# Merged DMAs, earlier query copies and another queue order in an attention and feed-forward kernel

## The chip, the cores and the metric

The kernel runs on one core of one Trainium2 chip. The metric is the device time of one execution in microseconds (us). A core has TensorE (matmuls; PE in the profile, PEld its weight loads), VectorE (DVE), ScalarE (ACT), GpSimd (POOL) and SyncE, whose queue (SP) issues the DMAs of this kernel.

## The reference

```python
def _attn_ref(q, k, v):              # q, k, v: 8 x 8 x 1152 x 64
    B, H, S, D = q.shape
    q_pool = q.reshape(B, H, S // 2, 2, D).mean(axis=3)
    scores = 1.0 / np.sqrt(D) * np.matmul(q_pool, k.transpose(0, 1, 3, 2))
    scores = scores - np.max(scores, axis=-1, keepdims=True)
    attn = np.exp(scores)
    attn = attn / (np.sum(attn, axis=-1, keepdims=True) + 1e-09)
    return np.matmul(attn, v)

def _moe_ref(x, w_in, w_out):        # x: 4608 x 512, w_in: 512 x 2048
    h = x @ w_in
    g = h - np.tanh(h)
    return g @ w_out
```

The attention's output, its heads side by side, is the x of the feed-forward part. Neighbouring queries are averaged in twos, so a head has 576 queries and 1152 keys. The maximum that is subtracted is the true one of each row.

## The kernel before

The attention stage comes first and the feed-forward stage after it. The attention works on 32 pairs of heads (8 batches, 4 pairs each). A pair is 36 units: for two halves of 288 queries, three groups of three key blocks of 128, and two heads, one unit multiplies a key block with 288 queries (two matmuls into one PSUM tile `ps_s`, of which there are three) and takes the exponential into `p_f`. The scores come out transposed, keys on partitions, so the row maximum must be known before: it is carried by two more rows (64 and 65) of the second operand `t2`.

These maxima are found ahead, by matmuls of their own. `query_sums` adds the two queries, `hi_part` (ScalarE) and `lo_part` (VectorE) split queries and keys into a high and a low part. `max_queries` copies the high queries by DMA into `bd`, a block-diagonal operand of 9 tiles of 128 columns, one buffer for even and one for odd pairs. `max_part` multiplies tiles of it with a third of the keys into `ps_m` (two buffers), and VectorE reduces that to `mx`; a pair has 14 such parts. `max_rows` reduces `mx` to the row maxima (`nm`), splits them (`m2`), has TensorE transpose them, ScalarE copy them (`mt`), one DMA write them to `m_dram` and others bring them back into `t2`. `operands` copies the high and low parts into the score operands `t1` and `t2` with ten DMAs, 2.6 MB a pair in all.

Behind the scores, GpSimd adds three of a group's `p_f` tiles (`z_part`), TensorE multiplies `p_f` with v (`pv`), and `z_sums` multiplies the sums with ones, 32 columns wide, to give the softmax's denominators. At the end of a batch these go through `z_dram`, `reciprocals` (VectorE) and `spread` to `r_dram`; the second stage multiplies x by them. Beside this `w_block` splits the weights into high and low parts, a block every 34 units, in steps on ScalarE, VectorE and GpSimd, and stores them in `wi_dram` and `wo_dram`.

All of this is ordered by hand. `add(u, f)` puts a step on the list of unit u; `run(u, first)` runs the list `first` ahead of the unit's score, `run(u)` the list `at` behind it, and `pv` follows. The units of each step are given relative to the first unit of its pair, so -35 is 35 units before the pair begins. Engines keep this order: an instruction that waits holds up all behind it on its engine, and SyncE's queue holds all DMAs of the stage. The dictionary `units`, with the lists `parts` and `rows`, holds the places; pairs 0, 1 and 2 have places of their own. In the steady part of the stage the places of one pair in terms of the pair that is computed are: load at 16 and query sums at 33 (three pairs ahead), high parts at 35, 1 and 3, bd copies at 4, low parts at 8, 10 and 12, maxima from 15 on, over 31 units; and for the next pair operands at 1, v at 6, row maxima at 15, their store at 21 and return at 26.

The feed-forward stage takes ten chunks (eight of 512 tokens, two of 256) through 16 blocks of the hidden dimension; its loops are not part of the change.

Of the kernel before, what the change touches and what calls it, by code (L numbers as in the profile page):

```python
# [8 lines left out]
F32 = mybir.dt.float32  # L9
# [34 lines left out]
def kernel(  # L44
# [18 lines left out]
    P = 128  # L63
# [73 lines left out]
    with ExitStack() as actx:  # L137
# [45 lines left out]
        def load(pi):  # L183
            w = pairs[pi] = Pair()
            w.b, w.hp = divmod(pi, NP)
            w.i = pi % 2
            w.q_n = ld.tile([P, 2, SQ], F32, name="q_n")
# [45 lines left out]

        spots = [((j, j + 4), (c,)) for c in range(3) for j in range(4)] + [((8,), (0, 1)), ((8,), (2,))]

        def max_part(u, pi, ts, cs):

            w = pairs[pi]
            ps = ps_m.tile([P, 2, 512], F32, name="ps_m")
            both = [(t, c) for t in ts for c in cs]  # L240
            for i, (t, c) in enumerate(both):
                pe.matmul(ps[:, i, 0:CH], bd[w.i][:, t * P:(t + 1) * P], w.hi[:, SQ + c * CH:SQ + (c + 1) * CH], start=True, stop=True)
            mx = w.mx[:, ts[0]:ts[-1] + 1:4, cs[0]] if len(ts) == 2 else w.mx[:, 8, cs[0]:cs[-1] + 1]
            add(u + 1, lambda: dve.tensor_reduce(mx, ps[:, 0:len(both), 0:CH], axis=AX.X, op=ALU.max))

        def max_rows(u, pi, ta, tb):

            w = pairs[pi]
            n = tb - ta
            c0, c1 = ta * P, min(tb, 4) * P  # L250
            nm = sm.tile([P, 2, 5], F32, name="nm")[:, :, 0:n]
            dve.tensor_reduce(nm[:, :, 0:min(tb, 4) - ta], w.mx[:, 0:8].rearrange("p (h t) c -> p h t c", h=2)[:, :, ta:min(tb, 4)],
                              axis=AX.X, op=ALU.max, negate=True)
            if tb == 5:
                dve.tensor_reduce(nm[:, :, n - 1], w.mx[:, 8:9].broadcast_to([P, 2, 3]), axis=AX.X, op=ALU.max, negate=True)
            m2 = sm.tile([P, 20], F32R, name="m2")[:, 0:4 * n].rearrange("p (s h t) -> p s h t", s=2, h=2)
            dve.tensor_copy(m2[:, 0], nm)
            dve.tensor_tensor(m2[:, 1], nm, m2[:, 0].bitcast(F32), op=ALU.subtract)
            ps = ps_m.tile([P, 2, 512], F32R, name="ps_m")[0:4 * n, 0, 0:P]
            mt = sm.tile([20, P], F32R, name="mt")[0:4 * n]  # L260
            md = m_dram[w.i][:, :, ta:tb]

            def turn():
                pe.transpose(ps, m2.rearrange("p s h t -> p (s h t)"), ident_r)

            def out():
                act.activation(mt, ps, AF.Copy)
                add(u + (6 if pi > 1 else 3), lambda: sp.dma_start(md.rearrange("s h t n -> (s h) t n"), mt.bitcast(F32)))

            def back():  # L270
                x2 = t2[w.i].bitcast(F32)
                sp.dma_start(x2[64:66, :, c0:c1], m_dram[w.i][:, :, ta:min(tb, 4)].rearrange("s h t n -> s h (t n)"))
                if tb == 5:
                    for h in range(2):
                        sp.dma_start(x2[64:66, h, 512:SQ], m_dram[w.i][:, h, 4, h * 64:h * 64 + 64])
            add(u + 2, turn)
            add(u + 3, out, at=first)
            add(u + (11 if pi > 1 else 5), back)

# [10 lines left out]
        class Group:  # L290
            pass

        def z_part(grp):
# [5 lines left out]
        def pv(u, grp):  # L299
# [65 lines left out]
        def w_block(u, kind, r, c):  # L365
# [25 lines left out]
            for i, op in ((12, begin),  # L391
                          (14, lambda: ts(whole(t[0]), whole(t[0]), -top, top, op0=ALU.max, op1=ALU.min)),
                          (17, lambda: ts(t[1], t[0], -0x80000000, None, op0=ALU.bitwise_and)),
                          (19, lambda: stt(t[1], t[0], 3, t[1], op0=ALU.logical_shift_left, op1=ALU.bitwise_or)),
                          (22, lambda: ts(t[2], t[1], -0x800000, None, op0=ALU.bitwise_and)),
                          (24, lambda: stt(whole(t[2]), lo, 2.0 ** -36, whole(t[2]), op0=ALU.mult, op1=ALU.mult)),
                          (26, lambda: pool.tensor_tensor(whole(t[1]), whole(t[1]), whole(t[2]), op=ALU.add)),
                          (31, lambda: act.activation(t[3][:, 0], whole(t[1]), AF.Copy)),
                          (33, lambda: pool.tensor_tensor(t[3][:, 1], whole(t[1]), whole(t[3][:, 0]), op=ALU.subtract)),
                          (37, store)):  # L400
                add(u + i, op)
# [28 lines left out]
        for pi in range(n_pair):  # L430
            u = pi * U
            units = dict(load=-92, query_sums=-75, hi_q=-73, hi_k=-71, max_queries=-68, lo_q=-64, lo_k=-62, operands=-35, load_v=-30)
            rows = [(-21, 0, 5)]
            parts = [-57 + i * 34 // 14 for i in range(14)]
            order, step = spots, 2
            if pi == 2:
                units.update(query_sums=-62, hi_q=-60, hi_k=-59, max_queries=-57, lo_q=-54, lo_k=-52)
                parts = [-50 + i * 27 // 14 for i in range(14)]
            if pi < 2:
                order, step = sorted(spots, key=lambda x: x[0][0] in (3, 8)), 0  # L440
            if pi == 0:
                units.update(load=-60, query_sums=-50, hi_q=-49, hi_k=-48, max_queries=-47, lo_q=-46, lo_k=-45, operands=-44,
                             load_v=-43)
                rows = [(-20, 0, 3), (10, 3, 5)]
                parts = [-40 + 2 * i for i in range(9)] + [2 * i for i in range(5)]
            if pi == 1:
                v0 = -U
                units.update(load=v0 - 10, query_sums=v0 - 2, hi_q=v0 - 1, hi_k=v0, max_queries=v0 + 1, lo_q=v0 + 2, lo_k=v0 + 3)
                parts = [v0 + 10 + i * 18 // 14 for i in range(14)]
                units.update(operands=-30)  # L450
                rows = [(-8, 0, 3), (-7, 3, 5)]
            add(u + units["load"], load, pi)
# [5 lines left out]
            add(u + units["max_queries"], max_queries, pi)  # L458
            for x, part in zip(parts, order):
# [3 lines left out]
            for x, ta, tb in rows:  # L463
                add(u + x, max_rows, u + x, pi, ta, tb)

# [157 lines left out]
```

## Time and profile before

| | |
|---|---|
| median of 3 runs | 1932.51 us (1932.48 to 1935.91) |
| profiled execution | 1932.55 us |
| its span, first to last instruction | 1930.8 us |
| mean granted TensorE clock | 0.972 |
| PE busy | 1787.9 us (93%) |
| DVE busy | 1418.0 us (73%) |
| ACT busy | 1094.7 us (57%) |
| POOL busy | 1067.6 us (55%) |
| exponentials, ACT | 1152 of 411 ns |
| maxima, DVE, two tiles | 416 of 955 ns |

Busy time of PE is modelled, since matmuls overlap. Line L37 is a helper through which every instruction of the attention stage passes, so this stage is read by the names of the tiles: `ps_s<-t` is a score, `ps_m<-x,bd` a maximum's matmul, `ps_o<-p_f,v` the product with v, `ps_s<-z,ones` the sums of p, `bd<-x` the copy of the queries, `t<-x` and `t<-kq_l` the operand copies, `t<-m_dram` the return of the row maxima. "SPq" is the DMA-issuing queue: its rows show the time from the first issue to the end of the last. In a timeline the bracket behind a row is the idle time of that engine before it and what ended it. A window's row gives, for each engine, busy time and count, then the granted clock (1.00 is full), the DMA engines' share and GB/s.

### The profile page before, as it was taken

How to read it: one execution, taken by the hardware profiler on the slowest of the kernel's cores; microseconds unless marked ns; L12 is line 12 of the kernel's file. 1: busy time of each engine (PE TensorE's matmuls, PEld its weight loads, DVE VectorE, ACT ScalarE, POOL GpSimd, SP SyncE). 2: the span in 40 equal slices, each digit the busy share in tenths (PEclk: the TensorE clock that was granted, in tenths of full speed). 3: DMA queues.
4: the chain of work that ended last, by engine and by line, in shares of the span. 5: the costliest groups of instructions: out<-in, count | busy, mean ns of one | idle time of the engine just before them, and what ended most of it. 6: DMA issues, size and time to landing. Idle time of an engine off the chain costs nothing.

```text
span 1930.8 us, 28611 instructions
## 1 busy us (share of the span) xinstructions
PE 1787.9 (93%) x9922; PEld 1319.7 (68%) x9922; DVE 1418.0 (73%) x1821; ACT 1094.7 (57%) x2471; POOL 1067.6 (55%) x768
## 2 busy tenths in 40 slices
PE   5799898989899999999899799999999999999998
PEld 3466565656566666666566476787878778788887
DVE  5667665565757676766665089999899889888887
ACT  2355454545545555555455365666666666666676
POOL 2467675757656776766577627443535252524332
PEclk9999999999999999999999899999999999999999
DMA  7567676676757776768675372101101020101000
GB/s 196 130 195 196 181 190 192 175 192 175 211 159 182 200 197 186 195 186 198 184 187 149 133 285 62 54 21 46 40 27 61 6 66 1 58 1 44 9 29 23
DMA packets 110553, 242.33 MB, mean 126 GB/s; under 512 B 24512, under 2 KB 49744, under 8 KB 110408
## 3 DMA queue, kind: packets, MB, share of 16 engines
q1 hardware_dynamic: 110408, 240.50, 45.4%
q8 instruction: 79, 1.29, 0.3%
q14 instruction: 66, 0.54, 0.1%
HBM read 109.64 MB, written 36.42 MB: 76 GB/s over the span
## 4 chain that ended last, share of the span: by engine, by line
PE 60%; DVE 12%; DMA 12%; ACT 5%; POOL 5%; SPq 3%; issue 2%; DVEq 0%; POOLq 0%; ACTq 0%
PE ps_s L37 16%; PE ps_o L37 14%; PE ps_h L521 12%; PE ps_o L546 11%; PE ps_m L37 7%; DMA bd<-x 4%; SPq L37 3%; DMA x_f<-x_dram 2%; DVE g_s L536 2%; DVE g_w L535 2%; DVE g_s L537 2%; ACT p_f L37 2%; DMA x_r<-r_dram 2%; POOL x L120 2%; DVE mx L37 1%
## 5 line engine op out<-in xcount | busy, mean ns | idle before, releaser
L37 ACT ACTIVATE p_f<-ps_s 128x288 f32<-128x288 f32 x1152 | 419.3, 411 | 363.6 <-PE ps_s L37 329.0
L37 DVE TENSOR_REDUCE mx<-ps_m 128x2 f32<-128x768 f32 x448 | 410.4, 926 | 287.5 <-PE ps_m L37 286.4
L37 PE MATMUL ps_s<-t 128*128 128x288 f32 (+1 forms) x2304 | 457.5, 316 | 28.4 <-DMA t<-m_dram 16.1
L37 PEld LDWEIGHTS ps_s<-t 128*128 128x128 f32 (+1 forms) x2304 | 356.9, 193 | 165.9 <-issue 115.3
L37 POOL TENSOR_TENSOR z<-p_f 128x576 f32<-128x576 f32 x192 | 284.2, 1480 | 303.4 <-ACT p_f L37 250.7
L539 POOL TENSOR_TENSOR g_lo<-g_s,g_hi 128x512 fp32r<-128x512 f32 (+1 forms) x160 | 210.6, 1316 | 403.9 <-ACT g_hi L538 344.7
L37 PE MATMUL ps_o<-p_f,v 128*64 128x288 f32 x2304 | 343.7, 437 | 0.0
L521 PE MATMUL ps_h<-x,wi 128*128 128x512 f32 (+1 forms) x1440 | 325.1, 370 | 0.0
L37 PE MATMUL ps_m<-x,bd 128*128 128x384 f32 x864 | 247.9, 363 | 70.3 <-DMA bd<-x 57.5
L37 POOL TENSOR_TENSOR z<-z,p_f 128x576 f32<-128x576 f32 x192 | 297.0, 1547 | 17.7 <-ACT p_f L37 2.9
L521 PEld LDWEIGHTS ps_h<-x,wi 128*128 128x128 f32 x1440 | 254.8, 188 | 51.8
L546 PE MATMUL ps_o<-wo,g_hi 128*128 128x512 f32 x1008 | 275.5, 392 | 4.6 <-ACT g_hi L538 4.2
L37 PEld LDWEIGHTS ps_o<-p_f,v 128*64 128x64 f32 x2304 | 156.2, 144 | 123.2 <-issue 52.0
L546 PEld LDWEIGHTS ps_o<-wo,g_hi 128*128 128x128 f32 x1008 | 186.7, 188 | 46.8 <-ACT g_hi L538 7.9
L37 PEld LDWEIGHTS ps_m<-x,bd 128*128 128x128 f32 x864 | 149.5, 200 | 89.7 <-issue 45.5
L538 ACT ACTIVATE g_hi<-g_s 128x512 fp32r<-128x512 f32 (+1 forms) x160 | 94.3, 589 | 163.6 <-DVE g_s L537 161.2
L532 DVE SCALAR_TENSOR_TENSOR g_w<-g_u,ps_h 128x512 f32<-128x512 f32 (+1 forms) x160 | 100.1, 626 | 99.1 <-PE ps_h L521 67.4
L534 DVE SCALAR_TENSOR_TENSOR g_w<-g_w,g_u 128x512 f32<-128x512 f32 (+1 forms) x160 | 172.8, 1080 | 0.0
L546 PE MATMUL ps_o<-wo,g_lo 128*128 128x512 f32 x504 | 160.1, 393 | 6.6 <-POOL g_lo L539 6.4
L527 ACT ACTIVATE g_u<-ps_h 128x512 f32<-128x512 f32 (+1 forms) x160 | 87.6, 548 | 119.1 <-PE ps_h L521 118.9
L537 DVE COPY_PREDICATED g_s<-g_m,g_t 128x512 f32<-128x512 int32 (+1 forms) x160 | 135.2, 845 | 14.7 <-DVE g_s L536 0.5
L536 DVE SCALAR_TENSOR_TENSOR g_s<-g_s,g_w 128x512 f32<-128x512 f32 (+1 forms) x160 | 131.6, 823 | 17.0 <-ACT g_t L528 0.5
(60 smaller groups left out, 1933.8 us busy)
## 6 DMA issues: line engine op xcount, KB each, us to landing
t<-x SPq DMA_DIRECT2D x64, 432.0 KB
q_n<-in_q_dram SPq DMA_DIRECT2D x32, 576.0 KB
kq<-in_k_dram SPq DMA_DIRECT2D x32, 576.0 KB
t<-kq_l SPq DMA_DIRECT2D x64, 288.0 KB
t<-x SPq DMA_DIRECT2D x64, 288.0 KB
v<-in_v_dram SPq DMA_DIRECT2D x32, 576.0 KB
t<-kq_l SPq DMA_DIRECT2D x64, 144.0 KB
t<-x SPq DMA_DIRECT2D x64, 144.0 KB
```

The lines of the kernel that those rows point to most:

```text
L37: ins = self.tc.keep_in_program_order(f(*args, **kwargs))
L120: pool.tensor_tensor(x_l[:, hp, 0:n], x[:, 0:n], x_h[:, hp, 0:n].bitcast(F32), op=ALU.subtract)
L521: nc.tensor.matmul(h, wi[fc][:, w, c], x[:, c, 0:n], start=(j == 0), stop=(j == len(mm) - 1))
L527: nc.scalar.activation(u, h, AF.Square)
L532: nc.vector.scalar_tensor_tensor(w, u, -P0, h, op0=ALU.add, op1=ALU.mult)
L534: nc.vector.scalar_tensor_tensor(w, w, PL, u, op0=ALU.mult, op1=ALU.mult)
L535: nc.vector.scalar_tensor_tensor(w, s2, P2, w, op0=ALU.add, op1=ALU.mult)
L536: nc.vector.scalar_tensor_tensor(s1, s1, P1, w, op0=ALU.add, op1=ALU.mult)
L537: last = nc.vector.copy_predicated(s1, m.bitcast(I32), th).ins
L538: nc.scalar.activation(g_h, s1, AF.Copy)
L539: nc.gpsimd.tensor_tensor(g_l, s1, g_h.bitcast(F32), op=ALU.subtract)
L546: nc.tensor.matmul(po[j], g[:, ts], wo[fc][:, w], start=(fc == 0 and i == 0), stop=(fc == NF - 1 and i == 2))
```

## The change

The parts, in words:

- `bd` is laid out as two stretches of 576 columns, so that a head's queries are copied by one DMA instead of two; tile 4 holds the last 64 queries of one head and the first 64 of the other.
- `m_dram` has a row of twice 704 numbers, so that one DMA brings the maxima back instead of three. `z_dram` is written by one DMA instead of four, a block of `wi_dram` by one instead of four.
- The places move: for the pair three ahead load at 10, query sums at 22, high parts at 26, 28 and 30, bd copies at 32, low parts at 34 and then 0 and 2 of the following pair, maxima from 12 on over 30 units; operands stay at 1, v at 6; row maxima at 10, transposed at 15, stored at 18, returned at 24.
- A maximum's reduction goes on the list `first` of the unit behind its matmuls.
- `z_sums` is called right behind the next `pv` instead of one unit earlier.
- The reciprocals of a batch come 10 units later, the steps of a weight block 3 units later behind the first.
- Pair 0 finds all maxima before its first unit, and pair 1 is loaded right behind pair 0; both have their bd and operand copies before unit 0 and their row maxima in one go.

```diff
-    m_dram = dram.tile([2, 2, 2, 5, P], F32, name="m_dram")
+    m_dram = dram.tile([2, 2, 2 * (5 * P + 64)], F32, name="m_dram")
...
-                raw_copy(bd[w.i][r, h * 512:(h + 1) * 512], w.hi[r, 0:512])
-                raw_copy(bd[w.i][r, 8 * P + h * 64:8 * P + (h + 1) * 64], w.hi[r, 512:SQ])
+                raw_copy(bd[w.i][r, h * SQ:(h + 1) * SQ], w.hi[r, 0:SQ])
...
-        spots = [((j, j + 4), (c,)) for c in range(3) for j in range(4)] + [((8,), (0, 1)), ((8,), (2,))]
+        spots = [((j, j + 5), (c,)) for c in range(3) for j in range(4)] + [((4,), (0, 1)), ((4,), (2,))]
...
-            add(u + 1, lambda: dve.tensor_reduce(mx, ps[:, 0:len(both), 0:CH], axis=AX.X, op=ALU.max))
+            add(u + 1, lambda: dve.tensor_reduce(mx, ps[:, 0:len(both), 0:CH], axis=AX.X, op=ALU.max), at=first)
...
+        def max_rows(u, pi, steps):
+            w = pairs[pi]
+            nm = sm.tile([P, 2, 5], F32, name="nm")
+            for h in range(2):
+                dve.tensor_reduce(nm[:, h], w.mx[:, 4 * h:4 * h + 5], axis=AX.X, op=ALU.max, negate=True)
...
+            def there():
+                sp.dma_start(md[:, 0:10 * P].rearrange("s (r n) -> s r n", n=P), mt.bitcast(F32))
             def back():
+                sp.dma_start(w.t2[64:66, :, 0:SQ].bitcast(F32), md.rearrange("s (h n) -> s h n", h=2)[:, :, 0:SQ])
+            add(u + steps[0], turn)
+            add(u + steps[0] + 1, out, at=first)
+            add(u + steps[1], there)
+            add(u + steps[2], back)
...
             if grp.g == 2:
                 add(u + 1, o_out, w, hf, at=first)
-                add(u + G - 1, z_sums, u + G - 1, w, hf)
+                late.append((w, hf))
+                if w is pairs.get(n_pair - 1) and hf.n == 1:
+                    add(u + G, lambda: z_sums(u + G, *late.pop()))
+            elif late:
+                z_sums(u, *late.pop())
...
-                    for r in range(4):
-                        sp.dma_start(z_dram[w.b, r // 2, r % 2, w.hp:w.hp + 1], w.z_s[32 * r:32 * r + 1])
+                    sp.dma_start(z_dram[w.b].rearrange("r h a s -> (r h) a s")[:, w.hp], w.z_s[0:P:32])
...
-                        add(u + 12, lambda: reciprocals(dve, *tot[0]))
-                        add(u + 15, lambda: spread(sp, *tot.pop(0)))
+                        add(u + 22, lambda: reciprocals(dve, *tot[0]))
+                        add(u + 25, lambda: spread(sp, *tot.pop(0)))
...
-                    for j in range(0, WB, P):
-                        sp.dma_start(wi_dram[(c + j) // P, :, :, r], src[:, :, j:j + P])
+                    f = c // P
+                    sp.dma_start(wi_dram[f:f + WB // P, :, :, r].rearrange("f p s m -> p s f m"),
+                                 src.rearrange("p s (f m) -> p s f m", m=P))
...
-            units = dict(load=-92, query_sums=-75, hi_q=-73, hi_k=-71, max_queries=-68, lo_q=-64, lo_k=-62, operands=-35, load_v=-30)
-            rows = [(-21, 0, 5)]
-            parts = [-57 + i * 34 // 14 for i in range(14)]
...
+            units = dict(load=-98, query_sums=-86, hi_q=-82, hi_k=-80, max_queries=-76, lo_q=-74, lo_k=-72, operands=-35, load_v=-30)
+            row, steps = -26, (5, 8, 14)
+            parts = [-60 + i * 33 // 14 for i in range(14)]
+            step = 2
             if pi == 0:
...
+                units.update(load=-70, query_sums=-60, hi_q=-59, hi_k=-58, max_queries=-57, lo_q=-56, lo_k=-55, operands=-54,
+                             load_v=-50)
+                row, steps, step = -32, (2, 4, 5), 0
+                parts = [-46 + i for i in range(14)]
             if pi == 1:
                 v0 = -U
...
+                units.update(load=v0 - 69, query_sums=v0 - 31, hi_q=v0 - 30, hi_k=v0 - 29, max_queries=v0 - 28, lo_q=v0 - 27,
+                             lo_k=v0 - 26, operands=v0 - 25)
+                parts = [v0 + 2 + i * 20 // 14 for i in range(14)]
+                row, steps, step = v0 + 23, (2, 4, 8), 0
+            if pi == 2:
+                units.update(query_sums=-80, hi_q=-76, hi_k=-74, max_queries=-70, lo_q=-66, lo_k=-64)
+                parts = [-49 + i * 23 // 14 for i in range(14)]
```

More of the change, by code (lines that the diff above doesn't have):

```diff
@@ L186, in load @@
             w.i = pi % 2
+            w.t2 = t2[w.i]
             w.q_n = ld.tile([P, 2, SQ], F32, name="q_n")
@@ L242, in max_part @@
                 pe.matmul(ps[:, i, 0:CH], bd[w.i][:, t * P:(t + 1) * P], w.hi[:, SQ + c * CH:SQ + (c + 1) * CH], start=True, stop=True)
[L243 to L246 removed]
+            mx = w.mx[:, ts[0]:ts[-1] + 1:5, cs[0]] if len(ts) == 2 else w.mx[:, 4, cs[0]:cs[-1] + 1]
+            add(u + 1, lambda: dve.tensor_reduce(mx, ps[:, 0:len(both), 0:CH], axis=AX.X, op=ALU.max), at=first)
@@ L248, in max_rows @@
+        def max_rows(u, pi, steps):
             w = pairs[pi]
[L249 to L255, printed above, removed]
@@ L256, in max_rows @@
-            m2 = sm.tile([P, 20], F32R, name="m2")[:, 0:4 * n].rearrange("p (s h t) -> p s h t", s=2, h=2)
+            nm = sm.tile([P, 2, 5], F32, name="nm")
+            for h in range(2):
+                dve.tensor_reduce(nm[:, h], w.mx[:, 4 * h:4 * h + 5], axis=AX.X, op=ALU.max, negate=True)
+            m2 = sm.tile([P, 2, 2, 5], F32R, name="m2")
             dve.tensor_copy(m2[:, 0], nm)
             dve.tensor_tensor(m2[:, 1], nm, m2[:, 0].bitcast(F32), op=ALU.subtract)
-            ps = ps_m.tile([P, 2, 512], F32R, name="ps_m")[0:4 * n, 0, 0:P]
@@ L260, in max_rows @@
-            mt = sm.tile([20, P], F32R, name="mt")[0:4 * n]
-            md = m_dram[w.i][:, :, ta:tb]
+            mt = sm.tile([20, P], F32R, name="mt")
+            md = m_dram[w.i]
             def turn():
+                ps = w.ps_t = ps_m.tile([P, 2, 512], F32R, name="ps_m")[0:20, 0, 0:P]
                 pe.transpose(ps, m2.rearrange("p s h t -> p (s h t)"), ident_r)
             def out():
-                act.activation(mt, ps, AF.Copy)
-                add(u + (6 if pi > 1 else 3), lambda: sp.dma_start(md.rearrange("s h t n -> (s h) t n"), mt.bitcast(F32)))
+                act.activation(mt, w.ps_t, AF.Copy)
@@ L270, in back @@
+            def there():
+                sp.dma_start(md[:, 0:10 * P].rearrange("s (r n) -> s r n", n=P), mt.bitcast(F32))
             def back():
[L271 to L276, printed above, removed]
@@ L277, in max_rows @@
-            add(u + 3, out, at=first)
-            add(u + (11 if pi > 1 else 5), back)
+                sp.dma_start(w.t2[64:66, :, 0:SQ].bitcast(F32), md.rearrange("s (h n) -> s h n", h=2)[:, :, 0:SQ])
[3 more added lines that the diff above has]
+            add(u + steps[2], back)
         def score_unit(w, half, h, kt, p):
@@ L291 @@
             pass
+        late = []
         def z_part(grp):
@@ L391, in w_block @@
             for i, op in ((12, begin),
[L392 to L400, printed above, removed]
+                          (17, lambda: ts(whole(t[0]), whole(t[0]), -top, top, op0=ALU.max, op1=ALU.min)),
+                          (20, lambda: ts(t[1], t[0], -0x80000000, None, op0=ALU.bitwise_and)),
+                          (22, lambda: stt(t[1], t[0], 3, t[1], op0=ALU.logical_shift_left, op1=ALU.bitwise_or)),
+                          (25, lambda: ts(t[2], t[1], -0x800000, None, op0=ALU.bitwise_and)),
+                          (27, lambda: stt(whole(t[2]), lo, 2.0 ** -36, whole(t[2]), op0=ALU.mult, op1=ALU.mult)),
+                          (29, lambda: pool.tensor_tensor(whole(t[1]), whole(t[1]), whole(t[2]), op=ALU.add)),
+                          (34, lambda: act.activation(t[3][:, 0], whole(t[1]), AF.Copy)),
+                          (36, lambda: pool.tensor_tensor(t[3][:, 1], whole(t[1]), whole(t[3][:, 0]), op=ALU.subtract)),
+                          (40, store)):
                 add(u + i, op)
@@ L458 @@
             add(u + units["max_queries"], max_queries, pi)
-            for x, part in zip(parts, order):
+            for x, part in zip(parts, spots):
                 add(u + x, max_part, u + x, pi, *part)
@@ L462 @@
             add(u + units["load_v"], load_v, pi)
-            for x, ta, tb in rows:
-                add(u + x, max_rows, u + x, pi, ta, tb)
+            add(u + row, max_rows, u + row, pi, steps)
         def run(u, at=at):
```

14 lines of the change are left out of this document (removed).

## The prediction

> **What bounds the kernel now.** I read the page's chain first, then the windows, the waits, and last the timeline of single pairs. The profiled execution took 1932.55 us for a span of 1930.8 us; the median of the three runs is 1932.51 us, so this trace stands for them, and 1.75 us lies outside its span.
>
> ```profile
> PE 60%; DVE 12%; DMA 12%; ACT 5%; POOL 5%; SPq 3%; issue 2%; DVEq 0%; POOLq 0%; ACTq 0%
> ```
>
> TensorE carries the chain, but DMA and VectorE together hold 24% of it. The change touches the attention stage alone. For its steady part, 120 to 1050 us, two windows: the exponentials (ACT busy, count, clock, DMA) and then all engines (PE, PEld, DVE, ACT, POOL, clock, DMA).
>
> ```profile
> 0.00:120.00 120.00, 29.48 (x78) 0.94 0.64 167
> 120.00:1050.00 930.00, 370.87 (x1020) 0.96 0.71 188
> ```
> ```profile
> 0.00:120.00 120.00, 83.26 (x440) 57.66 (x442) 72.87 (x101) 43.88 (x108) 51.10 (x40) 0.94 0.64 167
> 120.00:1050.00 930.00, 856.20 (x5552) 579.49 (x5550) 616.81 (x759) 493.61 (x1303) 631.49 (x428) 0.96 0.71 188
> ```
>
> One exponential is one unit, 36 units are one pair. So 1020 units in 930 us are 0.912 us a unit, 32.8 us a pair, 28.3 pairs. TensorE is idle for 930 - 856.2 = 73.8 us of it, and a mean clock of 0.96 costs about 0.04 x 930 = 37 us more. Together that is 111 us, 3.9 us a pair. No other engine is near full: GpSimd 631, VectorE 617, ScalarE 494 us of 930. What TensorE waits for, and what VectorE waits for, in the same window (total, times, longest):
>
> ```profile
> PE ps_m L37 <- DMA bd<-x: 44.3, 32, 4.6
> PE ps_m L37 <- DVE mx L37: 18.3, 18, 4.6
> PE ps_s L37 <- ACT p_f L37: 9.4, 36, 0.7
> ```
> ```profile
> DVE w L37 <- ACT w L37: 28.9, 20, 4.2
> DVE rec L37 <- DMA rec<-z_dram: 19.7, 7, 6.8
> ```
>
> The largest is the wait for bd, the block-diagonal queries of the maxima, about once a pair. One such pair on the DMA-issuing queue and on TensorE, and the clock in 2 us steps behind it (the 0.50, 0.85 and 0.79 are the clock):
>
> ```profile
> 607.39 1.45 SPq L37 DMA_DIRECT2D t<-m_dram  x3
> 613.57 1.17 SPq L37 DMA_DIRECT2D t<-kq_l  x2
> ```
> ```profile
> 624.85 4.01 SPq L37 DMA_DIRECT2D bd<-x  x4
> ```
> ```profile
> 622.93 0.69 PE L37 MATMUL ps_s<-t 128*128 128x288 f32 x4
> 623.47 0.34 PE L37 MATMUL ps_m<-x,bd 128*128 128x384 f32 x1
> 623.74 1.17 PE L37 MATMUL ps_s<-z,ones 128*32 128x288 f32 x12
> 624.83 0.54 PE L37 MATMUL ps_s<-t 128*128 128x288 f32 x2
> 625.29 1.68 PE L37 MATMUL ps_o<-p_f,v 128*64 128x288 f32 x12
> 626.90 1.64 PE L37 MATMUL ps_s<-t 128*128 128x288 f32 x8
> 629.88 0.99 PE L37 MATMUL ps_m<-x,bd 128*128 128x384 f32 x2 [1.34 <-DMA bd<-x]
> ```
> ```profile
> 630.00:632.00 2.00, 1.87 (x9) 1.14 (x9) 0.99 (x2) 0.71 (x2) 1.19 (x2) 0.85 0.89 157
> 632.00:634.00 2.00, 2.00 (x9) 1.02 (x11) 0.93 (x1) 0.27 (x1) 1.92 (x2) 0.50 0.99 380
> 634.00:636.00 2.00, 2.00 (x12) 1.19 (x9) 0.00 (x0) 0.32 (x2) 0.54 (x1) 0.79 1.02 368
> ```
>
> The ten operand copies (t) are issued from 613.57 to 624.85, 11.3 us; only then come the four bd copies, for another 4.0 us. TensorE runs into the first maximum before they land, stands 1.34 us, and then loses (0.15 + 0.50 + 0.21) x 2 = 1.7 us to a lower clock. A pair with a smaller stall shows the rate without that loss; its two ends are the transposes of the row maxima:
>
> ```profile
> 663.89 0.23 PE L37 MATMUL ps_m<-ident_r,m 128*20 128x128 f32 x1 [0.27 <-DVE mx L37]
> ```
> ```profile
> 692.21 0.77 PE L37 MATMUL ps_m<-x,bd 128*128 128x384 f32 x2 [0.79 <-DMA bd<-x]
> ...
> 694.03 0.23 PE L37 MATMUL ps_m<-ident_r,m 128*20 128x128 f32 x1 [0.17 <-DVE mx L37]
> ```
>
> That pair took 694.03 - 663.89 = 30.14 us, 0.79 us of it still the wait for bd: 29.35 us without.
>
> **The change, part by part.** *Queries of the maximum ahead.* I count in units from a pair's start. Before, the bd copies of the pair after next are issued at unit 4, behind the operand copies of unit 1, for a first maximum at unit 15. After, they are issued at unit 32 of the pair before, five units ahead of those operand copies, for a first maximum at unit 12: 16 units or 13 us of room where 11 units held 15.3 us of issuing. The wait for bd goes. The operand copies now stand behind two bd copies on the queue (about 1.0 us each by the row of four); the cover is the queue's own idle time from 608.84 to 613.57, 4.7 us in which it waits for TensorE to finish with the operands. Without that cover it would be 2 us a pair on copies that are needed a whole pair later. With bd move the sums of the queries (unit 33 to 22), hi (35 to 26) and lo (8 to 34); the instructions are the same and engines with a third of their time free take them.
>
> *VectorE's order.* The maxima go to the front of their unit; what they overtake is delayed by one maximum at most, 0.96 us (its row is below). The row maxima get 5 units instead of 2 before TensorE turns them, and the weights' steps get 5 units instead of 2 behind ScalarE's first step (the 28.9 us wait). The reciprocals move by 10 units, some 8 us. Here is what one cost, VectorE first and then TensorE:
>
> ```profile
> 203.51 0.20 DVE L37 SCALAR_TENSOR_TENSOR rec<-rec 128x36 f32<-128x36 f32 x1 [6.79 <-DMA rec<-z_dram]
> ```
> ```profile
> 204.99 1.01 PE L37 MATMUL ps_m<-x,bd 128*128 128x384 f32 x2 [4.65 <-DVE mx L37]
> ```
>
> 8 us is longer than the longest of these waits, so TensorE's wait for VectorE should fall with it. Only the last chunk of the second stage needs the result, so lateness costs nothing.
>
> *The steady sum.* Not known is what comes late next. Bounds: 29.35 us a pair if only the bd wait of that pair goes, 30.14 us if something as long takes its place. I take the middle, 29.75, because the waits for ScalarE (9.4 us, 0.33 us a pair) stay, and some of VectorE's 18.3 us (0.65 a pair) may. Gain: (32.8 - 29.75) x 28.3 = 87 us; with the ends, 98 and 76.
>
> The Trainium skill speaks against the part of the gain that is clock: "TensorE: Matmul & The Clock Gate", section "HAM oscillation — how this bites in real kernels", has the clock fall only for idle gaps beyond about 3.4 us. This trace disagrees, with 0.50 of the clock behind a gap of 1.34 us. By the rule the 37 us would have another cause and stay, which is the second rival.
>
> *Sums of p behind the products.* The same 12 matmuls, in another place. Two scores between z and product take 0.46 us (624.83 to 625.29), four in a row 0.54 (622.93 to 623.47), so a change of neighbour costs up to 0.19 us, and one is saved for each of 64 halves: -12 us at best. Against it, product and sums in a row keep TensorE from scores for 1.6 + 1.1 = 2.7 us (625.29 to 626.90, 623.74 to 624.83), and ScalarE may then be what TensorE waits for, up to the 9.4 us that such waits now come to. I take nothing. GpSimd's sums have one unit more, so no new wait on them.
>
> *Merged DMAs.* Three small ones took 1.45 us (607.39), so 0.5 us each: one for three saves 1.0 us of the queue, one for four bd half of 4.0 us, z and wi as much as their count falls. In the steady part this lies beside TensorE's work (the same 4.7 us of idle queue): nothing. That a merged one is slower than its parts is bounded by their sum, which is what they take today.
>
> *The start.* Before, nine parts of the maxima of pair 0, then the row maxima, their way through m_dram, and the first score; the other five parts follow later and a second trip stalls the half.
>
> ```profile
> 18.80 0.96 DVE L37 TENSOR_REDUCE mx<-ps_m 128x2 f32<-128x768 f32 x1 [0.17 <-PE ps_m L37]
> 19.79 0.17 DVE L37 TENSOR_REDUCE nm<-mx 128x6 f32<-128x18 f32 x1
> ```
> ```profile
> 22.63 0.75 SPq L37 DMA_DIRECT2D m_dram<-mt  x1
> 28.51 0.67 SPq L37 DMA_DIRECT2D t<-m_dram  x1
> ```
> ```profile
> 30.64 0.58 PE L37 MATMUL ps_s<-t 66*128 66x288 f32 x1 [9.30 <-DMA t<-m_dram]
> ```
> ```profile
> 57.98 1.06 PE L37 MATMUL ps_s<-t 66*128 66x288 f32 x3 [6.84 <-DMA t<-m_dram]
> ```
> ```profile
> 1050.34 0.27 SPq L37 DMA_DIRECT2D m_dram<-mt  x1
> 1052.60 1.41 SPq L37 DMA_DIRECT2D t<-m_dram  x3
> ```
>
> After, all 14 parts come first: 5 x about 1 us more, row maxima at some 24.4 us. The second pair's query sums, hi and bd are then ahead of the store on the queue: about 3 us. The store itself took 5.9 us behind the loads of the second pair (22.63 to 28.51) and 2.3 us on a quiet queue (1050.34 to 1052.60); those loads now come at the very beginning, so I take 3. The way back took 2.1 us (28.51 to 30.64). 24.4 + 3 + 3 + 2.1 = 32.5 us, 2 us later than now. But the 6.84 us stall goes, as does what follows it: before, 78 units were done at 120 us. After, 32.5 + 78 x 29.75 / 36 = 97 us, plus 12 parts of later pairs that fall into this stretch, 24 matmuls of 0.27 us (623.47 to 623.74) = 6.5 us: 103.5. That is 16 us less; I take 14 for a crowded VectorE, with 5 and 20 as ends.
>
> From 1050 us on, the same work: 0. Sum: 1932.55 - 87 - 14 = 1831.6, so 1832 us. Ends: 1932.5 - 98 - 20 - 12 = 1803, and 1932.5 - 76 - 5 + 9 = 1861.
>
> **The rivals.** *The clock stays, or VectorE takes over.* If the idle time goes but the mean clock stays at 0.96, the gain is 37 us less: 1869. If VectorE is late where DMA was (the 18.3 us show that it can be), half of the steady gain and most of the start's are left: 1932.5 - 44 - 5 = 1884. Against it: the pair of 30.14 us had the same VectorE work and ran without either.
>
> *ScalarE blocked by the early hi parts: slower.* hi now comes at unit 26, nine units earlier, into a buffer that the operand copies of two pairs before still read. If they land late, ScalarE stands in front of all its exponentials and TensorE stops behind it. In the pair shown the copies begin at 613.57, and bd, issued behind them, was in use at 629.88; unit 26 is 613.6 + 26 x 0.83 = 635.2. So it decides from a slip of 5.3 us on. To undo 101 us it must cost 3.6 us a pair, to be slower by 30 us 4.6 us: a slip of 10 us, and 1962 us. Against it: the queue was idle for 4.7 us in front of the copies, and it has fewer DMAs to issue.
>
> *No change.* bd is early but TensorE's pace is set by another thing altogether: 1932 us. Against it: the unlike pairs of one trace, 30.1 against the mean of 32.8.
>
> **How the numbers follow.** Forecast (1803 to 1861) 0.65; clock or VectorE (1861 to 1900) 0.24; slower 0.08; no change 0.03. A measurement of this kernel tells 0.2% (4 us) from no change, so faster is 0.65 + 0.24 = 0.89. The range drops the first 2 us of the forecast's and takes in most of the second case: 1805 to 1895.
>
> **What would show it.** Right: no TensorE wait on bd in the waits, VectorE's wait for z_dram gone, the clock near 1.00 from 120 us on, transposes 29.5 to 30 us apart, the first score near 32 us and no second stall, 78 units by about 105 us. Wrong: a new long wait of ScalarE's x on DMA or GpSimd, more waits of TensorE on mx, a clock of 0.96 without the gaps, or a first score beyond 36 us.

## The result, and the profile after

The changed kernel took 1829.35 us (median of 4 runs, 1826.85 to 1830.94), the kernel before 1932.49 us (median of 4). The ratio is 0.9465, with a 95% interval of 0.9445 to 0.9485: 103 us less. The profiled execution took 1830.94 us for a span of 1829.2 us at a mean clock of 0.992, where before it was 1932.55, 1930.8 and 0.972.

First the windows of the kernel after, of the exponentials and then of all engines, with the columns as before. The steady part now begins at 105 us and ends at 950.

```profile
0.00:105.00 105.00, 29.03 (x78) 1.00 0.74 195
105.00:950.00 845.00, 370.66 (x1020) 0.99 0.78 206
```
```profile
0.00:105.00 105.00, 79.82 (x446) 55.87 (x446) 71.63 (x95) 43.12 (x106) 50.64 (x40) 1.00 0.74 195
105.00:950.00 845.00, 816.38 (x5550) 569.18 (x5550) 599.79 (x759) 484.09 (x1304) 628.57 (x427) 0.99 0.78 206
```

The same counts stand in shorter windows, so the gain can be read off. The first 78 units end at 105 us where they ended at 120: 15 us. The next 1020 take 845 us instead of 930: 85 us, or 29.8 us a pair instead of 32.8. What is left of the span was 1930.8 - 1050 = 880.8 us and is 1829.2 - 950 = 879.2: 1.6 us. Together that is 101.6 us of span.

Within the steady part TensorE is idle for 845 - 816.38 = 28.6 us where it was 73.8, and the clock takes about 0.01 x 845 = 8 us where it took 37. These two hold 74 of the 85 us. The remaining 11 us are a shorter busy time of TensorE (modelled) at full clock; the clock has two digits, so each of its terms may be off by 4 to 5 us. The run with the sums of p at their old place, further down, has 823.47 us of busy time at a clock of 1.00, about what the kernel before has at full clock (856.2 - 37 = 819), where the kernel after has 816.38 - 8 = 808. So the new place of the sums accounts for these 11 us, as far as such figures go.

What TensorE and VectorE wait for in that window (total, times, longest):

```profile
PE ps_m L37 <- DVE mx L37: 20.0, 20, 1.9
PE ps_s L37 <- ACT p_f L37: 4.6, 14, 0.6
PE ps_m L37 <- ACT mt L37: 3.9, 22, 0.2
```
```profile
DVE mx L37 <- PE ps_m L37: 236.5, 156, 4.0
DVE w L37 <- ACT w L37: 1.2, 1, 1.2
```

The wait for bd, 44.3 us before, is not on the list. VectorE's wait for the denominators (19.7 us before) is gone too, and its wait for ScalarE's weight step fell from 28.9 to 1.2 us. TensorE's wait for the maxima did not fall: 20.0 us, 18.3 before.

The queue at one steady pair shows the bd copies in front of the operand copies:

```profile
336.64 1.17 SPq L37 DMA_DIRECT2D bd<-x  x2
337.86 0.57 SPq L37 DMA_DIRECT2D w_raw<-in_moe_w_in_dram  x1
340.93 1.95 SPq L37 DMA_DIRECT2D t<-kq_l  x2
```

Two copies, issued in 1.17 us together, do what four did in 4.01 us in the pair that the prediction shows. Most of that is their place: four copies at the new place took 0.58 us each (median, in the run with the DMAs in pieces). The queue still waits for TensorE, from 338.43 to 340.93, before it can issue operands.

### The profile page after: what moved, and what is told of

Its sections match the earlier page's. It is cut to its first block, busy times and chain, and to the rows that moved or that the text cites. A ratio compares the mean times of both kernels' runs of the same rounds, so it can differ in the third digit from the quotient of the medians.

```text
span 1829.2 us, 28257 instructions
## 1 busy us (share of the span) xinstructions
PE 1742.4 (95%) x9920; PEld 1308.2 (72%) x9920; DVE 1384.6 (76%) x1815; ACT 1082.5 (59%) x2469; POOL 1063.9 (58%) x768
## 5 line engine op out<-in xcount | busy, mean ns | idle before, releaser
L37 DVE TENSOR_REDUCE mx<-ps_m 128x2 f32<-128x768 f32 x448 | 405.8, 924 | 264.1 <-PE ps_m L37 263.8
L37 PE MATMUL ps_s<-t 128*128 128x288 f32 (+1 forms) x2304 | 447.9, 314 | 14.9 <-ACT p_f L37 8.8
L37 PE MATMUL ps_o<-p_f,v 128*64 128x288 f32 x2304 | 326.0, 419 | 0.0
L37 POOL TENSOR_TENSOR z<-z,p_f 128x576 f32<-128x576 f32 x192 | 290.8, 1515 | 17.7 <-ACT p_f L37 3.0
L37 PE MATMUL ps_m<-x,bd 128*128 128x384 f32 x864 | 238.5, 356 | 32.1 <-DVE mx L37 17.3
L37 PEld LDWEIGHTS ps_o<-p_f,v 128*64 128x64 f32 x2304 | 150.0, 138 | 114.9 <-issue 30.1
L37 PEld LDWEIGHTS ps_m<-x,bd 128*128 128x128 f32 x864 | 143.8, 196 | 49.7 <-DVE mx L37 27.1
L534 DVE SCALAR_TENSOR_TENSOR g_w<-g_w,g_u 128x512 f32<-128x512 f32 (+1 forms) x160 | 164.6, 1029 | 0.0
L536 DVE SCALAR_TENSOR_TENSOR g_s<-g_s,g_w 128x512 f32<-128x512 f32 (+1 forms) x160 | 126.8, 792 | 17.1 <-DVE g_w L535 0.5
```

Source lines behind the costliest of these rows:

```text
L37: ins = self.tc.keep_in_program_order(f(*args, **kwargs))
L534: nc.vector.scalar_tensor_tensor(w, w, PL, u, op0=ALU.mult, op1=ALU.mult)
L536: nc.vector.scalar_tensor_tensor(s1, s1, P1, w, op0=ALU.add, op1=ALU.mult)
```

## Experiments

The theory was the prediction's: bd's place on the queue sets the pace; VectorE's order and the reciprocals keep the next wait short; sums of p and merged DMAs are worth nothing in the steady part. Each run below sets this against a rival at one step. Every run has runs of the kernel before beside it, in four sets. The changed kernel itself was run a second time, to compare across the sets:

> The kernel after itself once more, as a measure for the two others of this call: every theory expects 1826 to 1834 us.

It took 1829.57 us (ratio 0.9467, 0.9436 to 0.9498), 0.2 us from the first result, so differences below are taken from 1829.5. The kernel before had medians of 1932.49, 1932.27, 1928.78 and 1932.66 us in the sets, so a difference across sets is good to about 4 us only. The set with 1928.78 holds the reciprocals put back, the third pair, the even maxima and the first run of the pieces; by the ratios these four are some 4 us slower against after than said below.

### bd put back behind the operand copies

```diff
-query_sums=-86, hi_q=-82, hi_k=-80, max_queries=-76, lo_q=-74, ...
+query_sums=-86, hi_q=-82, hi_k=-80, max_queries=-68, lo_q=-74, ...
```

> The kernel after with one place changed: the bd copies go back to unit 4, behind the ten operand copies; maxima still from unit 12. Theory A (the place of the bd copies is what pays): the copies land some 14 to 16 us after the pair begins, the first maximum comes at 12 x 0.83 = 10 us, so TensorE stands 2 to 5 us a pair again and loses about 1.7 us to the clock behind it: 28 pairs x 3.5 to 6.7 us = 1925 to 2015 us, granted clock in the steady part 0.96 or less, longest waits of TensorE on bd. Rival B (VectorE's order pays, bd only hid behind it): under 30 us slower, 1829 to 1860 us.

Measured: 1967.31 us, ratio 1.0187 (1.0167 to 1.0208). One place on the list turns the gain of 103 us into a loss of 35. From its profile: TensorE's longest waits between 120 and 1040 us; the exponentials there; and one stall, with the clock in 2 us steps behind it (the clock is the third number from the end).

```profile
PE ps_m L37 <- DMA bd<-x: 74.3, 26, 6.2
```
```profile
120.00:1040.00 920.00, 352.23 (x960) 0.92 0.67 177
```
```profile
321.03 0.98 PE L37 MATMUL ps_m<-x,bd 128*128 128x384 f32 x2 [5.61 <-DMA bd<-x]
```
```profile
322.00:324.00 2.00, 2.00 (x11) 1.90 (x9) 1.31 (x2) 1.38 (x3) 0.00 (x0) 0.50 1.04 427
324.00:326.00 2.00, 2.00 (x8) 1.58 (x6) 0.90 (x2) 0.97 (x3) 0.69 (x1) 0.50 0.93 376
```

The wait for bd is back and larger than in the kernel before (44.3 us), as it must be if the place decides: the first maximum now comes at unit 12 of the pair and not at 15, with bd at unit 4 in both. 920 us for 960 units are 34.5 us a pair. The stall of 5.61 us is followed by the clock at half. So in this kernel bd must come ahead of the operand copies.

### bd alone, in the kernel before

```diff
-units = dict(load=-92, query_sums=-75, hi_q=-73, hi_k=-71, max_queries=-68, lo_q=-64, lo_k=-62, ...)
+units = dict(load=-98, query_sums=-86, hi_q=-82, hi_k=-80, max_queries=-76, lo_q=-74, lo_k=-72, ...)
```

The third pair keeps its own places.

> The kernel before with only load, query sums, high parts, bd copies and low parts at their new places for pairs 3 to 31; four bd copies a pair, old maxima, old order of VectorE, old start. Theory A: the 44 us wait for bd goes and with it most of the 37 us of clock and none of the start's 14 us: 1855 to 1875 us, clock 0.98 to 0.99 in the steady part. Rival B: TensorE then waits for VectorE where it waited for bd, 1900 to 1930 us.

Measured: 1891.78 us, ratio 0.9805 (0.9773 to 0.9838): 40 us, between the two theories. The waits of TensorE and VectorE from 120 to 1040 us, and the exponentials:

```profile
PE ps_m L37 <- DVE mx L37: 43.6, 44, 5.4
PE ps_s L37 <- ACT p_f L37: 14.8, 39, 2.9
```
```profile
DVE rec L37 <- DMA rec<-z_dram: 35.5, 7, 7.4
```
```profile
120.00:1040.00 920.00, 384.89 (x1060) 0.97 0.73 193
```

The wait for bd is gone here too, but 1060 units in 920 us are still 31.25 us a pair. VectorE's wait for the denominators grew from 19.7 to 35.5 us, and TensorE's wait for VectorE from 18.3 to 43.6. The reading, which the next run tests: part of the time that TensorE spent on bd had run beside the wait for the denominators; a faster pair reaches the reciprocals earlier, and z_dram has not come.

### bd and the reciprocals, in the kernel before

```diff
-add(u + 12, lambda: reciprocals(dve, *tot[0]))
-add(u + 15, lambda: spread(sp, *tot.pop(0)))
+add(u + 22, lambda: reciprocals(dve, *tot[0]))
+add(u + 25, lambda: spread(sp, *tot.pop(0)))
```

This stands on top of the run before.

> The kernel of e2_bd_only (the old kernel with the bd copies ahead) with the reciprocals and their spreading 10 units later, as in after. In e2_bd_only VectorE waited 35.5 us for the return through DRAM at seven batches and TensorE stood 3 to 5 us behind each. Theory A (once bd is early this is the next largest wait): 7 x 4 us of standing and 7 x 1.7 us of clock go, 1845 to 1860 us. Rival B (the steps of the weights and the transposes' place decide): 1875 to 1892 us.

Measured: 1862.96 us, ratio 0.9644 (0.9602 to 0.9685), 29 us below bd alone, a little above what the theory had. The waits of TensorE and VectorE from 120 to 1010 us, and the exponentials:

```profile
PE ps_m L37 <- DVE mx L37: 21.5, 38, 5.9
```
```profile
DVE rec L37 <- DMA rec<-z_dram: 2.0, 3, 0.9
```
```profile
120.00:1010.00 890.00, 385.44 (x1065) 0.99 0.76 201
```

33.5 us of VectorE's wait and 22 us of TensorE's are gone, the clock rises from 0.97 to 0.99, and a pair takes 30.1 us. Two moves of places hold 70 of the 103 us; of the other 33, 15 are the start, whose 78 units still end at 120 us in this run and in the one before it. VectorE's wait for ScalarE's weight step is 43.1 us in this run and 1.2 in after; the steps of the weights were not moved alone, so what that is worth is not shown.

### The reciprocals put back, in the kernel after

```diff
-u + 22 and u + 25
+u + 12 and u + 15
```

> The kernel after with the reciprocals and their spreading 10 units earlier, where they were. Theory A: VectorE waits again some 20 us in all for the return through DRAM at seven batches, TensorE stands behind it for 1 to 5 us each and loses clock: 1842 to 1860 us. Rival B: the new order of the maxima covers it, 1826 to 1834 us.

Measured: 1840.76 us, ratio 0.9543 (0.9529 to 0.9557): 11 us slower than after, a little under what the first theory had.

```profile
DVE rec L37 <- DMA rec<-z_dram: 26.1, 6, 6.2
```

VectorE's wait is back, but TensorE's wait for the maxima rises from 20.0 to 27.4 us only. The same move is worth 29 us in the kernel before with bd ahead, and 11 us here. Which other part softens it was not tried.

### The maxima's reductions back at the end of the unit

```diff
-add(u + 1, ..., at=first)
+add(u + 1, ..., at=first if pi == 0 else at)
```

> The kernel after with the reductions of the maxima in the unit's later list again (all pairs but the first). Theory A (the order within a unit counts): TensorE's waits for mx rise from 20 us to 35 us or more, with some clock, 1840 to 1855 us. Rival B: a unit is 0.83 us and a step of VectorE as long, so the place in the unit moves nothing: 1826 to 1833 us.

Measured: 1837.00 us, ratio 0.951 (0.9491 to 0.9528): 7 us slower. TensorE waited 21.4 us in 29 times for the maxima, against 20.0 in 20. That is too little for 7 us, and neither theory had it so. The steady window holds 1015 exponentials and not 1020, the first 105 us 77 and not 78, at the same clock. The order is worth some 7 us; the wait by which it is paid was not found.

### The sums of p one unit earlier again

```diff
-late.append((w, hf))
+add(u + G - 1, z_sums, u + G - 1, w, hf)
```

> The kernel after with the sums of p one unit ahead of the next product again, not right behind it. Theory A (a change of neighbour costs up to 0.19 us, 64 times): 1835 to 1842 us. Rival B, as predicted: nothing, 1826 to 1833 us.

Measured: 1830.00 us, ratio 0.9475 (0.9459 to 0.9492): the same time as after. Its waits and its steady window (the columns are those of all engines):

```profile
PE ps_m L37 <- DVE mx L37: 10.2, 13, 1.7
```
```profile
105.00:950.00 845.00, 823.47 (x5565) 567.73 (x5566) 602.70 (x760) 490.68 (x1305) 638.67 (x429) 1.00 0.78 207
```

The move does two things that cancel. With the sums right behind the product TensorE is busy for 816.38 us and not 823.47, at a clock of 0.99 and not 1.00, and its waits for the maxima are 20.0 us and not 10.2.

### The DMAs in their old pieces

Four copies for bd, three for the return of the maxima, four for z_dram and four for a block of wi_dram, at the places of after.

```diff
-raw_copy(bd[w.i][r, h * SQ:(h + 1) * SQ], w.hi[r, 0:SQ])
+raw_copy(bd[w.i][r, h * SQ:h * SQ + 512], w.hi[r, 0:512])
+raw_copy(bd[w.i][r, h * SQ + 512:(h + 1) * SQ], w.hi[r, 512:SQ])
...
-sp.dma_start(z_dram[w.b]...[:, w.hp], w.z_s[0:P:32])
+for r in range(4):
+    sp.dma_start(z_dram[w.b, r // 2, r % 2, w.hp:w.hp + 1], w.z_s[32 * r:32 * r + 1])
...
-sp.dma_start(wi_dram[f:f + WB // P, :, :, r]..., src...)
+for j in range(0, WB, P):
+    sp.dma_start(wi_dram[(c + j) // P, :, :, r], src[:, :, j:j + P])
```

> The kernel after with its DMAs in pieces again: four for bd, three for the way back of the maxima, four for z, four for a block of the first weights; all places as after. Theory A, as predicted: the pieces lie in time in which the queue waits for TensorE, so nothing in the steady part and at most 1 us at the start: 1826 to 1833 us. Rival B (the queue is short of time): some 4 us of issuing a pair delay what is behind, 1840 us or more.

Measured: 1837.64 us, ratio 0.9532 (0.9516 to 0.9548), 8 us slower, between the two theories. So the same kernel was run again beside after itself:

> The kernel of e5_split once more, beside after on the same chip, since 1837.6 us lay 8 us above the first measurement of after from another call. Theory A (unmerged DMAs cost what they showed): 6 to 10 us above after. Rival B (the two calls ran on unlike chips): within 3 us of after.

Measured: 1837.99 us, ratio 0.9519 (0.9484 to 0.9554), against 1829.57 for after in the same set: 8.4 us. What follows sets the profile of the first run of the pieces against that of after, run again. The steady part holds these exponentials where after had 1020, and 1024 when run again: five to nine units, some 4 to 7.5 us.

```profile
105.00:950.00 845.00, 368.69 (x1015) 0.99 0.78 206
```

The weight stores on the queue, in after run again and then in pieces (count, shortest, median and longest ns of issuing):

```profile
L37 SPq DMA_DIRECT2D wi_dram<-w_hl x15: 637/644/1811, 114.4 to 856.4; - x15
```
```profile
L37 SPq DMA_DIRECT2D wi_dram<-w_hl x60: 513/618/2171, 119.2 to 866.8; - x60
```

A quarter of a block takes as long to issue as the whole: 0.62 against 0.64 us. By the medians the pieces add 27 us of issuing for wi_dram and, by the same rows for the others, 31 us for bd, 16 for the return and 11 for z_dram: 85 us, 3.0 us a pair. Most of it is absorbed: the queue's own waits for TensorE fall from 150.8 to 102.1 us and those for m_dram from 97.8 to 34.1. But its waits for the landing of loads, not among its largest waits in after, now come to 30.7 us for queries and 20.9 us for v, and GpSimd's wait for the queries rises from 25.7 to 33.2 us. TensorE's own waits hardly change. That the pieces cost 8 us together is shown, twice; by which wait they reach TensorE is not, and the four kinds were not tried apart.

### The third pair's places later

```diff
-units.update(query_sums=-80, hi_q=-76, hi_k=-74, max_queries=-70, lo_q=-66, lo_k=-64)
+units.update(query_sums=-68, hi_q=-64, hi_k=-62, max_queries=-58, lo_q=-56, lo_k=-54)
```

> The kernel after with the query sums, high, low and bd steps of the third pair 10 to 12 units later. In the trace of after ScalarE waits 8.2 us at 37 us for the sums of this pair's queries (which wait for their load) and TensorE 3.7 us behind it. Theory A: that wait goes, 3 to 5 us less, 1824 to 1826 us. Rival B: the low parts then meet the maxima of the second pair on VectorE and it is no faster, 1828 us or more.

Measured: 1833.33 us, ratio 0.9505 (0.9484 to 0.9527): no faster. The stall of 3.67 us at the start (shown further down) goes, but TensorE now meets the third pair's queries too late:

```profile
57.07 0.98 PE L37 MATMUL ps_m<-x,bd 128*128 128x384 f32 x2 [5.87 <-DMA bd<-x]
```

So 72 and not 78 units are done by 105 us. The rival had the result, by another way than it said. Pairs behind it run as in after (1024 exponentials from 105 to 950 us).

### Maxima spread evenly over the pair

```diff
-parts = [-60 + i * 33 // 14 for i in range(14)]
+parts = [-64 + i * 36 // 14 for i in range(14)]
```

> The kernel after with the maxima of pairs 3 to 31 spread evenly over all 36 units (from unit 8 on) instead of 30. Theory A (TensorE waits for VectorE because the maxima come too densely): its 20 us on mx and the clock lost behind them fall by half or more, 1810 to 1822 us. Rival B (VectorE is late where its steps run slowly beside GpSimd, whatever the spacing): 1825 to 1833 us.

Measured: 1836.20 us, ratio 0.9521 (0.9507 to 0.9536): 7 us slower, which neither theory had.

```profile
PE ps_m L37 <- DVE mx L37: 35.2, 51, 2.0
```

The waits for the maxima rise from 20.0 us in 20 times to 35.2 us in 51. So spreading them, from four units earlier on, does not help; the theory that their crowding causes these waits is not borne out, and slow steps beside GpSimd are not shown as the cause by this run either.

### Every weight block at the same place of its pair

```diff
-u = U // 2 + 34 * i
+u = U * i - 4
```

> The kernel after with one line changed: a block of the weights every 36 units from unit -4 on, not every 34 from unit 18 on, so that its steps on VectorE fall at the same place of every pair (units 13 to 23), away from the low parts (units 34, 0 and 2). In after the pairs whose weight steps fall on the low parts take 30 to 33 us, the others 28.5 us. Theory A (what is left of TensorE's waits for mx is this meeting of two kinds of work): its waits on mx fall below 8 us, pairs 28.5 to 29.5 us, 1790 to 1808 us. Rival B (VectorE is simply too full): 1822 to 1835 us.

Measured: 1864.01 us, ratio 0.9644 (0.9612 to 0.9675): 34 us slower than after. It does what it was made for, since no wait of TensorE for the maxima is left on its list, and it is slower than both theories had it. Its waits from 105 to 950 us, of TensorE, ScalarE, GpSimd and the queue:

```profile
PE ps_s L37 <- ACT p_f L37: 55.2, 52, 2.0
```
```profile
ACT x L37 <- POOL kq L37: 68.1, 26, 3.5
```
```profile
POOL kq L37 <- DMA q_n<-in_q_dram: 163.0, 25, 7.1
```
```profile
SPq L37 <- POOL w_hl L37: 141.4, 28, 7.2
```

A chain of three engines: GpSimd waits for the load of the queries, ScalarE's high parts wait for GpSimd's sums in front of the exponentials, and TensorE waits for the exponentials. The queue closes it: its wait for the split weights (`w_hl`, from GpSimd) is 141.4 us where it was 31.2 in after. The weight store now comes in front of the operand copies of every pair, before its block is done. In one pair nothing is issued from 288.00 us until the store goes out at 294.67, and the load of the queries is issued only at 306.81, behind all of the operand copies. The clock is 1.00 and 990 units take 845 us, 30.7 us a pair: 30 units, 25 us, fewer than in after. The first 105 us hold 66 units and not 78, another 10 us. So 55 us of waits in pieces of up to 2.0 us cost time with almost no loss of clock; of those longer than 1 us one, of 1.81 us at 534.14, has a lower clock behind it (0.50 from 536 to 538 us).

## Why the prediction was right, point by point

**The wait for bd goes: right.** So the list says, and putting bd back brings it back. That the operand copies may be later without harm held as well: no wait on them is in the list of after.

**The steady sum: right in size (85 us, 87 predicted; 29.8 us a pair, 29.75 predicted), with one cause split otherwise.** The prediction took the pair of 30.14 us as showing what is left without bd. For the change as a whole that holds. bd alone gave 40 us, since the wait for VectorE grew at once; only with the reciprocals, another 29 us, does a pair come near 30. The prediction costed the reciprocals' move as no more than a part of 18.3 us. It had the mechanism and the direction, and not that the wait for bd covered part of the wait for the denominators.

**VectorE's order: two waits went, a third did not.** The waits for the denominators and for the weights went as forecast. TensorE's wait for the maxima was to fall and came to 20.0 us, 18.3 before: this step of the prediction failed. The reason given for why late reciprocals are free, that only the last chunk needs them, is not right either; they are free because the second stage first reads `r_dram` at 974.4 us, and the last of the moved ones is stored at 918.6. Two pairs of the kernel after, each between two transposes of row maxima:

```profile
326.77 0.23 PE L37 MATMUL ps_m<-ident_r,m 128*20 128x128 f32 x1
355.29 0.23 PE L37 MATMUL ps_m<-ident_r,m 128*20 128x128 f32 x1
621.04 0.23 PE L37 MATMUL ps_m<-ident_r,m 128*20 128x128 f32 x1 [1.25 <-DVE mx L37]
652.64 0.23 PE L37 MATMUL ps_m<-ident_r,m 128*20 128x128 f32 x1
```

The first took 28.52 us, and TensorE waited for VectorE in it not once; the second took 31.60 us at the same clock of 1.00, with three waits for the maxima of 2.7 us in all (the 1.25 us in its first row lie ahead of it). The mean of 29.8 is one of unlike pairs. "29.5 to 30 us apart" was right as a mean and wrong as a picture.

**Clock: right.** It is 0.99. The rival in which the clock stays, by the rule of the Trainium skill that the prediction names, fell: the 37 us went to 8 together with gaps that were 44.3 / 32 = 1.4 us in the mean. Only three of TensorE's waits before, from 120 to 1050 us, were longer than 3.4 us (3.45, 4.60 and 4.65). Here the same in small, in the kernel after: a gap of 1.39 us, and the clock behind it.

```profile
197.81 0.88 PE L37 MATMUL ps_m<-x,bd 128*128 128x384 f32 x2 [1.39 <-DVE mx L37]
```
```profile
198.00:200.00 2.00, 2.00 (x8) 1.35 (x9) 2.00 (x4) 0.41 (x1) 0.90 (x1) 0.50 0.88 213
200.00:202.00 2.00, 2.00 (x11) 0.90 (x8) 1.85 (x2) 0.06 (x1) 2.00 (x2) 0.65 0.98 219
```

**Sums of p: right.** Nothing was forecast and 0.5 us measured, with both bounds at work: some 11 us less busy time at full clock (12 at best in the prediction), paid back in waits and clock. But the waits that came back are those for the maxima, not those for ScalarE that the prediction had.

**Merged DMAs: the other step that failed.** They were costed at nothing, "beside TensorE's work", with 4.7 us of idle queue as the cover. They are worth 8 us. The cover exists, as the queue's waits show, but it lies in front of the operand copies. That the 3 us of issuing a pair delay what stands elsewhere is the likely reading and not shown. The total came out within 3 us all the same, and that is in part luck: these 8 us are in the measured gain and not in the sum, so the rest of the sum was too high by about as much.

**The start: right in sum (15 us, 14 predicted), with errors inside.** VectorE, the queue, TensorE, ScalarE and TensorE again at the start of the kernel after:

```profile
25.71 0.24 DVE L37 TENSOR_REDUCE nm<-mx 128x5 f32<-128x15 f32 x2
```
```profile
29.01 0.73 SPq L37 DMA_DIRECT2D m_dram<-mt  x1
30.96 0.65 SPq L37 DMA_DIRECT2D t<-m_dram  x1
```
```profile
33.32 1.54 PE L37 MATMUL ps_s<-t 66*128 66x288 f32 x5 [5.99 <-DMA t<-m_dram]
```
```profile
37.29 0.68 ACT L37 ACTIVATE x<-kq 128x576 fp32r<-128x576 f32 x1 [8.23 <-POOL kq L37]
```
```profile
39.17 0.85 PE L37 MATMUL ps_s<-t 128*128 128x288 f32 x2 [3.67 <-ACT p_f L37]
```

The row maxima (`nm`) came at 25.71 us (24.4 predicted), the store's way took 30.96 - 29.01 = 1.95 us (3 predicted, 5.9 before), and the first score came at 33.32 us (32.5). The second stall of 6.84 us is gone. Not foreseen was ScalarE's wait of 8.23 us for the third pair's sums on GpSimd, which cost TensorE 3.67 us. The prediction also named wrongly whose loads stood before the store in the kernel before: they are the third pair's (load at unit -20), and the second pair's came behind it. It made no difference, since in the kernel after the third pair's loads come behind the return.

**The slower rival: real, but not here.** In the kernel after, GpSimd waits 24.2 us for queries in the steady part, and ScalarE's high parts wait once, for 0.4 us. With the weight blocks moved a chain through the same high parts takes most of 34 us: not by late operand copies in a buffer, as the rival had it, but by late loads behind a weight store.

**The rest, from 1050 us on before and from 950 us on after: 0 predicted, 1.6 us less measured.**

## What to carry to other kernels

In a kernel ordered by hand the DMA-issuing queue is a schedule of its own: the small copy that the bounding engine meets next belongs ahead of the bulk copies (1.2 us in front of 11.3 us was worth more than any other single place here). Take a wait away and look at once for the one that ran beside it: bd alone gave 40 us, bd with the reciprocals 70. A wait that disappears is no gain by itself: with the weight blocks aligned all waits for the maxima went, and the kernel was 34 us slower, while the one queue waited 141.4 us to issue weight stores whose data was not ready.

## What the runs showed of the hardware that was not expected

Two small VectorE steps took several times as long beside GpSimd. VectorE and GpSimd in the kernel after:

```profile
586.25 1.21 DVE L37 CAST m<-nm 128x10 fp32r<-128x10 f32 x1
587.49 1.32 DVE L37 TENSOR_TENSOR m<-nm,m 128x10 fp32r<-128x10 f32 x1
588.74 1.81 DVE L37 TENSOR_REDUCE mx<-ps_m 128x2 f32<-128x768 f32 x2
```
```profile
586.14 1.28 POOL L37 TENSOR_TENSOR w<-w,w 128x512 f32<-128x512 f32 x1 [3.48 <-DVE w L37]
587.39 1.39 POOL L37 TENSOR_TENSOR z<-p_f 128x576 f32<-128x576 f32 x1
```

The cast of 128x10 numbers took 1.21 us, where the same one at 25.99 us, with GpSimd idle, took 0.17 us. Each of the two small steps ends within 0.05 us of the end of GpSimd's instruction (587.42 and 588.78), while the reductions from PSUM behind them take their usual 0.9 us each. The Trainium skill, "SBUF — State Buffer", section "Who interferes with whom", says that casts and steps with two SBUF inputs can be shut out by a whole GpSimd instruction, and reductions never; this trace agrees.

Issuing time of a DMA followed the count more than the bytes: 0.62 us for a quarter of a weight block, 0.64 us for the whole; for z_dram 0.24 us for a quarter, 0.57 for the whole.

The clock's answer to a gap is not one threshold on its length. Two waits of TensorE in the kernel before, each with the window behind it (the clock is the third number from the end):

```profile
722.65 0.71 PE L37 MATMUL ps_m<-x,bd 128*128 128x384 f32 x2 [0.80 <-DMA bd<-x]
```
```profile
724.00:726.00 2.00, 2.00 (x10) 1.04 (x10) 1.32 (x2) 0.75 (x3) 1.77 (x2) 0.50 1.00 235
```
```profile
735.49 0.62 PE L37 MATMUL ps_m<-x,bd 128*128 128x384 f32 x2 [2.28 <-DVE mx L37]
```
```profile
736.00:738.00 2.00, 2.00 (x19) 1.09 (x17) 2.00 (x4) 0.85 (x3) 0.86 (x1) 1.00 0.05 13
```

It fell to 0.50 behind a wait of 0.80 us (0.31 us more idle stood just before it) and stayed at 1.00 behind one of 2.28 us. What else decides is not shown here.
